# Attention and a mixture of experts on one core: the opening's order, and the gate weights' engine

## The chip, the cores and the metric

The kernel runs on one core of a Trainium2 chip. The core has TensorE (PE), VectorE (DVE), ScalarE (ACT), GpSimd (POOL) and SyncE (SP), which here only issues DMAs. Each engine works through its own instructions in the order in which the program lists them and waits at an instruction until the semaphores that it needs have come. The metric is the device time of one execution in microseconds, the median over runs.

## The reference

```python
# 2 batches x 8 heads, S = 1152, D = 64; q and k are 8 times a normal draw of 0.1
q_pool = q.reshape(B, H, S // 2, 2, D).mean(axis=3)          # 576 pooled queries
scores = np.matmul(q_pool, k.transpose(0, 1, 3, 2)) / np.sqrt(D)
attn = softmax(scores)                                         # with 1e-09 in the sum
x = np.matmul(attn, v)                                         # -> [1152 tokens, 512]
p = domain_probs / (domain_probs.sum(-1, keepdims=True) + 1e-09)
for e in range(4):                                             # all experts, dense
    out += p[:, e:e + 1] * (np.maximum(x @ w1[e], 0.0) @ w2[e])
```

## The kernel before

Two heads make a pair; there are eight pairs, and the pooled queries of a pair make nine **tiles** i = 0 to 8 of 128 rows, numbered through as g = 9n + i. The matmuls on q, k and the weights take fp32r operands, and to keep precision each operand is split into a high part `hi` (a rounded copy) and a low part `lo` (the value less `hi`). The split costs a copy and a subtraction for every operand, and which engine does them is one of the things that the change moves.

A tile goes through these steps, for which the text uses the letters:

- **S(g)**: six matmuls (nine for i = 8) in TensorE, three chunks of 384 keys into the one PSUM tile `spt` (L314). There is one `spt`, so S(g+1) can't begin before N(g) has read it.
- **N(g)**: VectorE negates and scales the scores into SBUF and takes the minimum (L317).
- **E(g)**: ScalarE's exponential with its sum (L323).
- **T(g)**: 18 half transposes of the exponentials in TensorE (L202, tile `pt`), two PSUM tiles from a pool of two; ScalarE copies the first out (L339), VectorE the second (L337).
- **PV**: TensorE's product with v (L352, tile `po`), spread over later tiles.

The main loop for tile g issues T(g), E(g+1), a part of PV, preparations, and then S(g+2) and N(g+2). The preparations for the next pair are `prep_q` (12 transposes, a copy by ScalarE, splits in POOL, four DMAs that stack `hi` and `lo`), and `prep_k` 1 and 2 (eight transposes each, a copy out of PSUM, a split in POOL, four DMAs). What `prep_k` transposes has first to be joined by POOL from the two heads' rows (`join_k`, L251, into `qsf` or `raw`). For the first pair the table `PREP0` puts them in tiles 2, 3 and 4, for later pairs `PREP` in tiles 0, 2 and 4. The PSUM pool of two (`ps_t`) that T uses is also that of these transposes.

Pair 0 has a way of its own. Its first four q blocks (the first **q chunk**) are added, transposed and split ahead of the k of the first head (`prep_q0(0)`, L222 and L223); the second chunk follows in tile 0 and the last block in tile 1, split by ScalarE and VectorE straight from PSUM. k is split in its row layout (`split_k0`, L228 and L229), transposed (L235) and copied out (L238). POOL adds the rest of q in one instruction (L177).

The gate weights p (`gate_weights`, L489 to L495, two pieces of 36 columns at the end) are computed once, after tile 13, by VectorE.

Order is written by hand: nothing moves instructions but the order of the code. DMAs go through SP's queue, also in that order. After the attention come the experts' matmuls (L135 and L669), in which TensorE is busy nearly all the time.

## Time and profile before

| what | us |
|---|---|
| median of 3 runs | 651.31 (650.85 to 651.96) |
| the profiled execution | 650.89 |
| its span in the trace | 649.1 |
| TensorE busy in the span | 628.1 |
| first 40 us: tiles 0 to 6 of pair 0 | see the rows below |

A row of the timeline gives the start and duration in us, the engine, the line of the program, the operation, what it writes and reads, and in brackets how long its engine stood idle before and what ended that. "DVE L317 [0.71 <-PE spt L314]" is then: VectorE idle for 0.71 us until TensorE's scores came. A row with x6 merges six instructions. A row of the windows gives for each engine the busy time in the stretch and the number of instructions, then the granted clock of TensorE as a share of 2.4 GHz.

### The profile page before, as it was taken

Reading aid. Unit: us, or ns where it says so; the run is one execution under the profiler, and the core shown is the slowest. Engines: PE = TensorE matmul, PEld = TensorE weight load, DVE = VectorE, ACT = ScalarE, POOL = GpSimd, SP = SyncE. Lnnn points to the kernel's source line nnn. Section 1 sums busy time; section 2 is a strip of 40 time slices with the busy share of each in tenths; the row PEclk is TensorE's granted clock in tenths of the full one; section 3 lists DMA queues with packets and bytes.
Section 4 is the critical chain, followed back from the end, with each engine's and each line's share of the span. In section 5 each row is a group of like instructions: output and inputs, shape, how many; then the busy total and the mean of one; then the engine's idle time right before and its main releaser. Section 6 shows DMA issues by size and latency. Waiting matters only on the chain.

```text
span 649.1 us, 12072 instructions
## 1 busy us (share of the span) xinstructions
PE 628.1 (97%) x4828; PEld 518.8 (80%) x4828; DVE 356.6 (55%) x544; ACT 306.9 (47%) x510; POOL 340.5 (52%) x398
## 2 busy tenths in 40 slices
PE   7599999999999999999999999999999999999997
PEld 6466667676776767798899899899899889989976
DVE  5466766566665666744544544544454454454454
ACT  4467677766666677461441351352243144135030
POOL 3335253436372478685844854774584484485140
PEclk8899999999999999999999999999999999999999
DMA  6744544636272621121211211212111121120105
GB/s 218 166 121 109 142 119 131 151 98 172 78 191 61 170 69 34 33 66 33 66 33 33 66 34 35 63 33 58 40 49 51 33 65 33 34 66 0 33 1 145
DMA packets 41782, 50.87 MB, mean 78 GB/s; under 512 B 3712, under 2 KB 27520, under 8 KB 41728
## 3 DMA queue, kind: packets, MB, share of 16 engines
q1 hardware_dynamic: 40928, 48.94, 28.1%
q10 hardware_dynamic: 800, 1.18, 0.5%
q8 instruction: 38, 0.62, 0.4%
q14 instruction: 16, 0.13, 0.1%
HBM read 30.97 MB, written 2.36 MB: 51 GB/s over the span
## 4 chain that ended last, share of the span: by engine, by line
PE 90%; DVE 4%; ACT 3%; issue 1%; POOL 1%; DVEq 0%; POOLq 0%; ACTq 0%
PE p L669 30%; PE spt L314 12%; PE po L352 12%; PE chy L135 11%; PE chx L135 8%; PE chz L135 8%; PE pt L202 7%; DVE sx L317 2%; ACT sx L323 2%; PE pr L370 1%; PE pk L202 1%; PE pq L202 1%; PE warm L445 1%; DVE acc L673 0%; ACT xr L598 0%
## 5 line engine op out<-in xcount | busy, mean ns | idle before, releaser
L669 PE MATMUL p<-w2s,hb 128*128 128x512 f32 (+1 forms) x870 | 199.2, 388 | 1.1 <-DVE acc L673 0.9
L669 PEld LDWEIGHTS p<-w2s,hb 128*128 128x128 f32 x870 | 161.8, 188 | 34.2 <-issue 1.3
L673 DVE SCALAR_TENSOR_TENSOR acc<-p,pw,acc 128x512 f32<-128x512 f32 (+1 forms) x136 | 101.5, 747 | 82.7 <-PE p L669 82.7
L317 DVE TENSOR_SCALAR_CACHE_REDUCE sx<-spt 128x1152 f32<-128x1152 f32 x72 | 97.7, 1357 | 78.5 <-PE spt L314 70.2
L116 POOL TENSOR_TENSOR kk<-kq,kk 128x512 fp32r<-128x512 f32 x64 | 72.5, 1161 | 117.9 <-ACT kk L108 117.9
L314 PE MATMUL spt<-kk,q2all 128*128 128x384 f32 x456 | 101.0, 358 | 3.7 <-DVE sx L317 3.2
L323 ACT ACTIVATE sx<-sx,mn 128x1152 f32<-128x1152 f32 x72 | 90.6, 1259 | 23.1 <-DVE sx L317 21.4
L314 PEld LDWEIGHTS spt<-kk,q2all 128*128 128x128 f32 x456 | 77.6, 192 | 20.1 <-DVE sx L317 16.3
L352 PE MATMUL po<-aT,vn 128*64 128x320 f32 (+1 forms) x576 | 86.2, 422 | 0.0
L600 POOL TENSOR_TENSOR hb<-xr,hb 128x576 fp32r<-128x576 f32 x48 | 68.6, 1432 | 21.9 <-ACT hb L599 21.9
L637 ACT ACTIVATE xr<-chx 128x576 f32<-128x576 f32 x15 | 9.8, 651 | 147.5 <-PE chx L135 147.5
L339 ACT ACTIVATE aT<-pt 128x640 f32<-128x640 f32 x72 | 50.7, 704 | 54.7 <-PE pt L202 54.7
L202 PEld LDWEIGHTS pt<-ident,sx 64*128 64x128 f32 x1296 | 46.7, 140 | 22.2 <-ACT sx L323 10.1
L202 PE MATMUL pt<-ident,sx 64*128 64x64 f32 x1296 | 57.1, 230 | 2.9 <-DVE aT L337 1.1
L135 PE MATMUL chx<-xa,kk 128*128 128x288 f32 x384 | 56.4, 296 | 1.3 <-ACT xr L514 0.5
L135 PEld LDWEIGHTS chx<-xa,kk 128*128 128x128 f32 x384 | 53.4, 189 | 3.3 <-ACT xr L514 1.0
L352 PEld LDWEIGHTS po<-aT,vn 128*64 128x64 f32 x576 | 35.4, 137 | 20.3 <-issue 0.7
L337 DVE COPY aT<-pt 128x512 f32<-128x512 f32 x72 | 49.2, 683 | 2.4 <-PE pt L202 2.3
L95 POOL TENSOR_TENSOR kq<-kq 128x256 f32<-128x256 f32 x64 | 45.8, 737 | 7.5 <-DMA kq<-in_moe_w_dram 6.3
L598 ACT ACTIVATE xr<-xr 128x576 f32<-128x576 f32 x48 | 32.9, 686 | 34.1 <-DVE xr L596 34.1
L135 PE MATMUL chy<-xb,kk 128*128 128x288 f32 x288 | 46.7, 298 | 0.1
L135 PE MATMUL chy<-q2all,kk 128*128 128x288 f32 x256 | 44.2, 295 | 0.0
(100 smaller groups left out, 671.7 us busy)
## 6 DMA issues: line engine op xcount, KB each, us to landing
kq<-in_moe_w_dram SPq DMA_DIRECT2D x64, 128.0 KB, 2.4
qsf<-in_moe_w_dram SPq DMA_DIRECT2D x16, 512.0 KB, 3.7
q2all<-q2all SPq DMA_DIRECT2D x28, 256.0 KB, 4.8
vn<-in_v_dram SPq DMA_DIRECT2D x8, 576.0 KB, 5.3
kk<-kk SPq DMA_DIRECT2D x28, 160.0 KB, 2.6
kq<-in_q_dram SPq DMA_DIRECT2D x7, 576.0 KB, 7.4
kq<-in_k_dram SPq DMA_DIRECT2D x7, 576.0 KB, 4.1
kk<-kk SPq DMA_DIRECT2D x28, 128.0 KB, 4.6
```

The costliest lines, as they stand in the source:

```text
L116: nc.gpsimd.tensor_tensor(flat(w1s[u % 2][:, 1, a:b]), flat(wf[:, a:b]), flat(w1s[u % 2][:, 0, a:b].bitcast(F32)), ALU.subtract)
L135: nc.tensor.matmul(chain[:, c, :CW], w1s[u % 2][:, a, WI[wo], kt, :], xop(xo, z, kt)[:, c * CW:(c + 1) * CW], start=(first and kt == 0 and ...
L202: nc.tensor.transpose(pt[:, a, j, :], src[r], ident[r, r])
L314: nc.tensor.matmul(spt[g][:, c, :NC], w, x, start=(j == 0), stop=(j == len(ops) - 1))
L317: nc.vector.tensor_scalar(sx[g % 3].rearrange("p (c x) -> p c x", c=3), spt.pop(g)[:, :, :NC], -INV, None, ALU.mult, ALU.min, accum_out=mn ...
L323: nc.scalar.activation(sx[g % 3], sx[g % 3], AF.Exp, bias=mn[g % 3], scale=-1.0, accum_out=sums[n % 2][:, i:i + 1])
L337: nc.vector.tensor_copy(dst, pt)
L339: nc.scalar.activation(dst, pt, AF.Copy)
L352: nc.tensor.matmul(po[h * HALF:(h + 1) * HALF, :w], vn[n % 2][:, h, kt, :], aT[grp][:, h, kt, :], start=(kt == 0), stop=(kt == KT - 1))
L600: nc.gpsimd.tensor_tensor(lo, c, hi.bitcast(F32), ALU.subtract)
L669: nc.tensor.matmul(pc, h[:, a, sl, ts_], w[:, b, sl, c0:c1], start=(m == 0), stop=(m == len(ops) - 1))
L673: nc.vector.scalar_tensor_tensor(ac, pc, pw[:, tt, e:e + 1], ac, ALU.mult, ALU.add)
```

## The change

Four things change, all in pair 0 but the last:

1. **Opening.** The split of k (first head) stands ahead of the split of q's first chunk in ScalarE and VectorE. The q transposes keep their place.
2. **Second q chunk and last block.** Blocks 4 to 8 are transposed together in tile 0 (ten transposes), copied to `raw` by VectorE in one piece, and split by POOL. Nothing of them is left in tile 1. The stacking DMAs, the sum of the next pair's q (`add_q`) and `join_k(0)` and `join_k(1)` follow S(2) in tile 0.
3. **Preparations for pair 1.** `PREP0` has tiles 3, 4 and 5 rather than 2, 3 and 4. `prep_q` no longer joins k rows for pair 1, and `prep_k` copies into a free part of `xr` rather than `raw`. The load of the k rows of pair 2 follows in tile 5.
4. **Gate weights.** The product and the two copies (L492, L495) run in POOL; the sum, the addition and the reciprocal stay in VectorE.

```diff
@@ -209,18 +209,26 @@
             nc.gpsimd.tensor_scalar(hi, src, 1.0, 1.0, ALU.mult, ALU.mult)
             nc.gpsimd.tensor_tensor(lo, src, hi.bitcast(F32), ALU.subtract)
 
-        def prep_q0(c):
-            ts_ = range(4 * c, min(4 * c + 4, 9))
-            pt = half_transposes("pq", [qs[:, t].rearrange("p z d -> p (z d)") for t in ts_], ps_s if c == 0 else None)
-            if c == 2:
-                for a, r in enumerate(ROWS):
-                    nc.scalar.activation(q2m[0][r, 0, r], pt[r, a, 0], AF.Copy)
-                for a, r in enumerate(ROWS):
-                    nc.vector.tensor_tensor(q2m[0][r, 1, r], pt[r, a, 0], q2m[0][r, 0, r].bitcast(F32), ALU.subtract)
-                return
-            hi, lo = [q2[0][:, z, :, 256 * c:256 * c + 256].rearrange("p s (t x) -> p s t x", x=HALF) for z in range(2)]
-            nc.scalar.activation(hi, pt, AF.Copy)
-            nc.vector.tensor_tensor(lo, pt, hi.bitcast(F32), ALU.subtract)
+        def transposes_q0(ts_, pool=None):
+            return half_transposes("pq", [qs[:, t].rearrange("p z d -> p (z d)") for t in ts_], pool)
+
+        def q_split(hi, lo, src):
+            nc.scalar.activation(hi, src, AF.Copy)
+            nc.vector.tensor_tensor(lo, src, hi.bitcast(F32), ALU.subtract)
+
+        def parts_q0(c):
+            return [q2[0][:, z, :, 256 * c:256 * c + 256].rearrange("p s (t x) -> p s t x", x=HALF) for z in range(2)]
+
+        def prep_q0():
+            pt = transposes_q0(range(4, 9))
+            src = raw[:, :10 * HALF].rearrange("p (a k x) -> p a k x", a=2, x=HALF)
+            nc.vector.tensor_copy(src, pt)
+            pool_split(*parts_q0(1), src[:, :, :4])
+            split_q2m(0, src)
+
+        def split_q2m(n, src):
+            for a, r in enumerate(ROWS):
+                pool_split(q2m[n % 2][r, 0, r], q2m[n % 2][r, 1, r], src[r, a, 4])
 
         def split_k0(h, c):
             t0, t1 = TCH[c]
@@ -275,16 +283,16 @@
                     dst = q2[n % 2].rearrange("p z s (y x) -> p (z s) y x", y=2)[r, :, y, :]
                     st = stq.rearrange("p z s j x -> p (z s) (j x)")[y * HALF:(y + 1) * HALF]
                     nc.sync.dma_start(dst.bitcast(F32), st.bitcast(F32))
-            for a, r in enumerate(ROWS):
-                pool_split(q2m[n % 2][r, 0, r], q2m[n % 2][r, 1, r], src[r, a, 4])
+            split_q2m(n, src)
             ab = kab[n % 2]
             pool_split(halves(ab[:, 0], 8, 9)[:, :, 0], halves(ab[:, 1], 8, 9)[:, :, 0], src[:, :, 5])
-            join_k(1)
+            if n > 1:
+                join_k(1)
 
         def prep_k(n, c):
             t0, t1 = KTS[c]
             pt = half_transposes("pk", [kc[c][:, (t - t0) * P:(t - t0 + 1) * P] for t in range(t0, t1)])
-            src = raw[:, :4 * P]
+            src = raw[:, :4 * P] if n > 1 else xr[:, 3, :4 * P]
             if c == 1:
                 join_k(2)
                 nc.vector.tensor_copy(halves(src, 0, 4), pt)
@@ -444,11 +452,12 @@
         for _ in range(NWARM):
             nc.tensor.transpose(warm[:, :P], ident, ident)
         add_q0(nc.vector, 0, 4)
-        prep_q0(0)
+        pq = transposes_q0(range(4), ps_s)
         split_k0(0, 0)
         ev = [prep_k0(0, 0)]
         split_k0(0, 1)
         ev.append(prep_k0(0, 1))
+        q_split(*parts_q0(0), pq)
         for fn in ev:
             fn()
         S_chunk(0, 0)
@@ -472,7 +481,7 @@
                  4: (0, 0, 0, 2), 5: (0, 0, 2, 4), 6: (0, 0, 4, 6), 7: (0, 0, 6, 8), 8: (0, 0, 8, 9)}
         SPREAD = {7: (0, 0), 1: (-1, 1)}
         PREP = {0: [(prep_q,)], 2: [(prep_k, 1)], 4: [(prep_k, 2)]}
-        PREP0 = {2: [(prep_q,)], 3: [(prep_k, 1)], 4: [(prep_k, 2)]}
+        PREP0 = {3: [(prep_q,)], 4: [(prep_k, 1)], 5: [(prep_k, 2)]}
 
         def pv_part(g):
             n, i = divmod(g, 9)
@@ -489,10 +498,10 @@
             nc.vector.tensor_reduce(prs, pr, AX.X, ALU.add)
             nc.vector.tensor_scalar_add(prs, prs, 1e-9)
             nc.vector.reciprocal(prs, prs)
-            nc.vector.tensor_tensor(pr, pr, prs.unsqueeze(2).to_broadcast([P, 18, E]), ALU.mult)
+            nc.gpsimd.tensor_tensor(pr, pr, prs.unsqueeze(2).to_broadcast([P, 18, E]), ALU.mult)
             for a in range(2):
                 sl = slice(a * HALF, (a + 1) * HALF)
-                nc.vector.tensor_copy(pw[sl], pr[sl, a:a + 17:2, :])
+                nc.gpsimd.tensor_copy(pw[sl], pr[sl, a:a + 17:2, :])
 
         for g in range(NTL):
             n, i = divmod(g, 9)
@@ -515,17 +524,12 @@
             pv_part(g)
             if i in SPREAD and n + SPREAD[i][0] >= 0:
                 spread_sums(n + SPREAD[i][0], SPREAD[i][1])
+            if g == 0:
+                prep_q0()
             if n + 1 < NP:
-                if g < 2:
-                    prep_q0(g + 1)
-                if g == 0:
-                    stack_k0()
-                if g == 1:
-                    add_q(nc.gpsimd)
-                    join_k(0)
                 for fn, *args in (PREP if n else PREP0).get(i, []):
                     fn(n + 1, *args)
-                if i == 4 and n + 2 < NP:
+                if i == (4 if n else 5) and n + 2 < NP:
                     load_kv(kn, k, n + 2)
             elif i == 7:
                 chx = ps_s.tile([P, 3, 512], F32, tag="s", name="chx")
@@ -535,6 +539,11 @@
                 for kt in range(2):
                     product(0, 2, kt, chx, False)
             scores(g + 2)
+            if g == 0:
+                stack_k0()
+                add_q(nc.gpsimd)
+                join_k(0)
+                join_k(1)
             if i == 3:
                 inv_sums(n, 0)
             if (n, i) == (1, 4):
```

ScalarE at the start of the program, first before and then changed (`kq` holds the rows of q and k, `kk` the split and transposed k, `q2all` the split q, `pq` and `pk` are PSUM tiles):

```order
L222 ACTIVATE q2all<-pq 128x2x256
L228 ACTIVATE kk_74<-kq 128x5x64
L228 ACTIVATE kk_74<-kq 128x4x64
L238 ACTIVATE kk_73<-pk 128x640
L228 ACTIVATE kk_74<-kq 128x5x64
```

```order
L236 ACTIVATE kk_74<-kq 128x5x64
L236 ACTIVATE kk_74<-kq 128x4x64
L216 ACTIVATE q2all<-pq 128x2x256
L246 ACTIVATE kk_73<-pk 128x640
L236 ACTIVATE kk_74<-kq 128x5x64
```

The high part of k now stands ahead of that of q; all else in the engine keeps its place.

TensorE in tiles 0 to 4 of pair 0, before and then changed (`pt<-ident,sx` is T, `spt` is S, `po` is PV, `pq` and `pk` are transposes of q and k):

```order
L202 MATMUL pt<-ident,sx_90 128x64 x18
L202 MATMUL pq<-ident,qsf 128x64 x8
L314 MATMUL spt<-kk_73,q2all 128x384 x6
L202 MATMUL pt<-ident,sx_91 128x64 x18
L202 MATMUL pq<-ident,qsf 128x64 x2
L314 MATMUL spt<-kk_73,q2all 128x384 x6
L202 MATMUL pt<-ident,sx_92 128x64 x18
L202 MATMUL pq<-ident,qsf 128x64 x10
L202 MATMUL pq<-ident,raw 128x64 x2
L314 MATMUL spt<-kk_73,q2all 128x384 x6
L202 MATMUL pt<-ident,sx_90 128x64 x18
L202 MATMUL pk<-ident,qsf 128x64 x8
```

```order
L202 MATMUL pq<-ident,qsf 128x64 x10
L322 MATMUL spt<-kk_73,q2all 128x384 x6
L202 MATMUL pt<-ident,sx_91 128x64 x18
L322 MATMUL spt<-kk_73,q2all 128x384 x6
L202 MATMUL pt<-ident,sx_92 128x64 x18
L322 MATMUL spt<-kk_73,q2all 128x384 x6
L202 MATMUL pt<-ident,sx_90 128x64 x18
L202 MATMUL pq<-ident,qsf 128x64 x10
L202 MATMUL pq<-ident,raw 128x64 x2
L322 MATMUL spt<-kk_73,q2all 128x384 x6
L202 MATMUL pt<-ident,sx_91 128x64 x18
L360 MATMUL po<-aT_93,vn_88 64x256 x4
```

Ten transposes of q stand in tile 0 (the second piece begins right behind T(0)), the preparation of pair 1's q is one tile later, and the first `pk`, which came after T(3), follows T(4) and its PV.

POOL after the sum of q's later blocks, before and then changed (64x64 are the two halves of the last q block, 128x128 into `kk` the ninth k block, `qsf<-kq 128x512` is `join_k`):

```order
L177 TENSOR_TENSOR qsf<-kq 128x640
L184 TENSOR_TENSOR qsf<-kq 128x2x4x64
L188 TENSOR_TENSOR qsf<-kq 128x128
L251 COPY raw<-kq 128x128
L209 TENSOR_SCALAR q2all<-raw 128x512
L210 TENSOR_TENSOR q2all<-raw,q2all 128x512
L209 TENSOR_SCALAR q2all<-raw 64x64
L210 TENSOR_TENSOR q2all<-raw,q2all 64x64
L209 TENSOR_SCALAR q2all<-raw 64x64
L210 TENSOR_TENSOR q2all<-raw,q2all 64x64
L209 TENSOR_SCALAR kk_74<-raw 128x128
L210 TENSOR_TENSOR kk_74<-raw,kk_74 128x128
```

```order
L177 TENSOR_TENSOR qsf<-kq 128x640
L209 TENSOR_SCALAR q2all<-raw 128x2x256
L210 TENSOR_TENSOR q2all<-raw,q2all 128x2x256
L209 TENSOR_SCALAR q2all<-raw 64x64
L210 TENSOR_TENSOR q2all<-raw,q2all 64x64
L209 TENSOR_SCALAR q2all<-raw 64x64
L210 TENSOR_TENSOR q2all<-raw,q2all 64x64
L184 TENSOR_TENSOR qsf<-kq 128x2x4x64
L188 TENSOR_TENSOR qsf<-kq 128x128
L259 COPY raw<-kq 128x128
L259 COPY qsf<-kq 128x512
L209 TENSOR_SCALAR q2all<-raw 128x512
```

Six instructions that split pair 0's own q are new at the front; `join_k(1)`, which stood behind the last row of the first list, now stands ahead of the splits of pair 1's q.

## Rows read from the trace of the kernel before

**Rows 1.** The page, part 1: busy us (share of the span) and instructions

```profile
PE 628.1 (97%) x4828; PEld 518.8 (80%) x4828; DVE 356.6 (55%) x544; ACT 306.9 (47%) x510; POOL 340.5 (52%) x398
```

**Rows 2.** Windows: each engine's busy us and instructions, PEclk granted, DMA share, GB/s

```profile
8.00:8.50 0.50, 0.15 (x1) 0.15 (x1) 0.50 (x1) 0.50 (x2) 0.50 (x1) 0.80 0.07 28
...
20.00:25.00 5.00, 4.00 (x56) 2.86 (x55) 3.43 (x6) 3.71 (x9) 0.21 (x1) 1.00 0.85 189
...
30.00:35.00 5.00, 5.00 (x38) 3.69 (x34) 2.98 (x6) 1.70 (x2) 2.90 (x4) 0.50 0.82 193
...
35.50:36.00 0.50, 0.50 (x11) 0.43 (x9) 0.00 (x0) 0.00 (x0) 0.00 (x0) 0.89 0.87 205
```

**Rows 3.** Timeline of the opening: start us, us, engine, line, tile, idle before

```profile
1.19 0.89 SPq L173 DMA_DIRECT2D kq<-in_k_dram  x2
...
5.17 0.60 ACT L222 ACTIVATE q2all<-pq 128x512 fp32r<-128x512 f32 x1 [3.16 <-PE pq L202]
...
5.66 0.77 ACT L228 ACTIVATE kk<-kq 128x320 fp32r<-128x320 f32 x2
...
6.40 0.82 DVE L229 TENSOR_TENSOR kk<-kq,kk 128x320 fp32r<-128x320 f32 x2
...
7.60 0.70 ACT L238 ACTIVATE kk<-pk 128x640 fp32r<-128x640 f32 x1 [1.17 <-PE pk L235]
...
7.94 0.69 DVE L238 CAST kk<-pk 128x512 fp32r<-128x512 f32 x1 [0.72 <-PE pk L235]
...
8.35 2.29 PE L314 MATMUL spt<-kk,q2all 128*128 128x384 f32 x6 [0.46 <-ACT kk L238]
...
10.68 1.36 DVE L317 TENSOR_SCALAR_CACHE_REDUCE sx<-spt 128x1152 f32<-128x1152 f32 x1 [0.71 <-PE spt L314]
```

**Rows 4.** DMA issues, window 1.15 to 1.3 us: KB, us to landing

```profile
kq<-in_k_dram SPq DMA_DIRECT2D x1, 288.0 KB, 3.1
```

**Rows 5.** Timeline, POOL in the opening

```profile
7.74 1.55 POOL L177 TENSOR_TENSOR qsf<-kq 128x640 f32<-128x640 f32 x1 [5.57 <-DMA kq<-in_q_dram]
```

**Rows 6.** Source view of L229: duration ns min/median/max

```profile
L229 DVE TENSOR_TENSOR kk<-kq,kk x4: 410/450/946, 6.4 to 9.6; 128x320 fp32r<-128x320 f32 x2, 128x256 fp32r<-128x256 f32 x2
```

**Rows 7.** Timeline of tiles 1 to 4, VectorE

```profile
13.72 1.36 DVE L317 TENSOR_SCALAR_CACHE_REDUCE sx<-spt 128x1152 f32<-128x1152 f32 x1 [1.07 <-PE spt L314]
...
16.99 0.69 DVE L223 TENSOR_TENSOR q2all<-pq,q2all 128x512 fp32r<-128x512 f32 x1 [1.30 <-ACT q2all L222]
...
21.19 1.36 DVE L317 TENSOR_SCALAR_CACHE_REDUCE sx<-spt 128x1152 f32<-128x1152 f32 x1
...
23.98 1.36 DVE L317 TENSOR_SCALAR_CACHE_REDUCE sx<-spt 128x1152 f32<-128x1152 f32 x1 [0.82 <-PE spt L314]
```

**Rows 8.** Timeline of tile 3, POOL and who waits

```profile
24.79 0.62 POOL L209 TENSOR_SCALAR q2all<-raw 128x512 fp32r<-128x512 f32 x1 [8.65 <-ACT raw L270]
...
25.49 1.27 POOL L210 TENSOR_TENSOR q2all<-raw,q2all 128x512 fp32r<-128x512 f32 x1
...
28.94 0.61 POOL L251 COPY qsf<-kq 128x512 f32<-128x512 f32 x1
...
29.60 0.69 PE L202 MATMUL pk<-ident,qsf 64*128 64x64 f32 x8 [4.38 <-POOL qsf L251]
```

**Rows 9.** Timeline, TensorE in tiles 5 and 7

```profile
37.17 0.78 PE L202 MATMUL pt<-ident,sx 64*128 64x64 f32 x18
...
45.53 1.29 PE L314 MATMUL spt<-kk,q2all 128*128 128x384 f32 x6
```

**Rows 10.** Timeline, gate weights

```profile
70.08 0.97 DVE L492 TENSOR_TENSOR pr<-pr,prs 128x72 f32<-128x72 f32 x1
...
72.24 0.47 PE L202 MATMUL pt<-ident,sx 64*128 64x64 f32 x8 [1.14 <-DVE aT L337]
```

**Rows 11.** DMA issues L263, windows 40.5 to 41 and 61.4 to 61.6 us

```profile
kk<-kk SPq DMA_DIRECT2D x1, 160.0 KB, 2.7
...
kk<-kk SPq DMA_DIRECT2D x1, 128.0 KB, 5.7
```

## The prediction

> **What bounds the kernel now.** The page first: TensorE is busy for 628.1 of 649.1 us [rows 1], so this change can only save idle time of TensorE and time at its lower clock. Both lie in the first pair. The windows of the granted clock come second: 1.00 (2.4 GHz) nearly everywhere, but falling to 0.50 (1.2 GHz) after 8.0, and 0.50 from 30 to 35 us, back at 35.5 to 36 [rows 2]. Third, the timeline of the opening, read for what each wait ends on. S(0) begins at 8.35, released by ScalarE's copy of the transposed k, and its six matmuls take 2.29 us at the low clock [rows 3] where S(9) takes 1.29 [rows 9]. In tiles 1 and 2 VectorE waits 1.30 us for ScalarE's half of the q split, and N(2) stands behind that [rows 7]. In tile 3 TensorE waits 4.38 us for `join_k(1)`, which POOL reaches only after all splits of pair 1's q [rows 8]; the low clock follows. From tile 5 on TensorE has hardly a gap, so a start that is earlier there is kept to the end. The one later gap that the change touches is 1.14 us behind the gate weights [rows 10].
>
> **Opening: k ahead of q.** The k rows of the first head land at 1.19 + 3.1 = 4.3 [rows 3, 4], but ScalarE takes them at 5.66, behind q's high part, which itself waits until 5.17 for TensorE [rows 3]. Changed, k's high part can run from 4.3 to 5.1 and its low part on VectorE (two times about 0.4) until 5.7; q's parts keep 5.17 and 5.8 to 6.5, as their wait is on TensorE. So the nine k transposes end at about 6.35 and no longer after 7.6. ScalarE's copy (0.70) follows q's high part, 6.0 to 6.7, and S(0) begins at 6.75: 1.6 us earlier. If the landing slips to 5.0, k's high part pushes q's back and 1.0 us is left; more than 1.6 isn't to be had, since q's high part waits for TensorE.
>
> TensorE was idle from 5.1, when ScalarE took over from it, to 6.9, when the first low part of k was done [rows 3], and then the clock fell. Now it is idle for some 0.3 us there and again 0.4 before S(0), so I take S(0) at full clock: another 1.0 us (2.29 against 1.29). N(0) then begins at 10.68 - 2.5 = 8.2. The bounds for the clock are 0 and 1.0; I take 1.0, as tiles 1 to 3 kept the full clock with TensorE busy for 4.00 of 5 us [rows 2], and the new opening is about as busy.
>
> **Second q chunk through POOL.** From N(0) to N(1) nothing changes (10.68 to 13.72, 3.05): N(1) at 11.25. N(1) to N(2) took 3.9 and N(2) to N(3) 3.6 us, each with a piece of q between; N(3) to N(4), with none, 2.79 [rows 3, 7]. That is the chain S, N, S through the one `spt`. Changed, tile 0 has ten transposes (0.4) ahead of S(2): N(2) at 14.4, N(3) 17.2, N(4) 20.0. VectorE's copy of 640 columns is new; nothing shows it, but ScalarE takes 0.70 for 640 and VectorE 0.69 for 512 [rows 3], so it lies between 0.7 and 0.9. It runs beside S(2) and costs nothing; if S(2) didn't cover it, 0.2. POOL's split (0.62 and 1.27 as in [rows 8]) ends at about 16.2 and is needed by S(4) at 18.6. Behind it POOL has some 4 us of work (q's last block, `add_q`, the two joins) until 20.2; the transposes of `prep_q` come at 21.4. Both are covered by more than a microsecond.
>
> **Joined k rows and the later preparations.** `pk` 1 finds its rows ready, so the 4.38 us wait goes, and with it the idle time ahead of the second low-clock stretch. `prep_q`'s 12 transposes stand ahead of S(5): N(5) at 23.4. Then TensorE is the bound: T(4) 0.78, PV about 1.0, `pk` 0.4, S(6) 1.3, and T(5) begins at 26.75, where it began at 37.17 [rows 9].
>
> What is late next is POOL. ScalarE's copy for `prep_q` ends at 23.7 (N(4), E(4) and 0.8). From the start of the splits to the join it took 4.15 us (24.79 to 28.94); one copy of 0.4 for the sums now stands ahead of `join_k(2)`, which ends at 23.75 + 4.15 + 0.4 + 0.6 = 28.9. TensorE wants `pk` 2 at 28.45, after T(5) and PV: a stall of 0.5. POOL's split of `pk` 1 (2.0 with its gaps) ends at 31.0; only then can ScalarE copy `pk` 2 into the same part of `xr` (0.6), and the second half of T(6), which needs the PSUM tile that this copy empties, waits until 31.7 where TensorE would be there at 31.1: 0.6. Queued behind that copy on ScalarE stands E(7), needed only 3 us later. Bounds of both stalls: 0 and, if POOL runs 10% slower over these 7 us, 1.9; I take 1.2 (rounded up).
>
> From T(5) to S(9) it took 8.36 us [rows 9]. Now `pk` 2 (0.4) and the stalls come to it: S(9) at 26.75 + 8.36 + 0.4 + 1.2 = 36.7 and not 45.53, **8.8 us earlier**. The stacking DMAs of `pk` 2, also a tile later, must not end after that: the second of them is issued at 33.8 and lands 2.7 later [rows 11], at 36.5, and S(9) reads what it brings in its second chunk, at 37.1. The load of pair 2's k rows, also queued a tile later on SP, keeps over 2 us ahead of its join.
>
> **Gate weights.** VectorE drops L492 (0.97) and two copies (0.4). The copy behind them moves from 71.5 to 70.1, and T(15)'s second half no longer waits 1.14 us for it: **1.25** with the hand-over. POOL takes three small instructions, at a time when what follows is not wanted for over 5 us.
>
> One row speaks against a part of the change, in the opening again. One of the four L229 took 946 ns, where the median is 450; the last of them starts at 9.6, so the long one lies beside POOL's L177, 7.74 to 9.29 [rows 5, 6]. Changed, L229 of the second head runs at 7.1 to 7.9, and its second piece begins at about 7.5, 0.25 us ahead of L177. If POOL comes first, that piece waits until 9.29 and N(0) with it: 1.55 us.
> The Trainium skill says as much (SBUF — State Buffer, "Who interferes with whom"): a VectorE instruction with two SBUF inputs and a GpSimd one that reads SBUF need the same port, and the one that begins first keeps it to its end. By that rule the trace's 946 ns is a blocked instruction, and the order of the two starts decides between the sum above and the second case below.
>
> **Sum.** 8.8 + 1.25 = 10.05. The profiled execution took 650.89 (its span of 649.1 and 1.8 around it, which stay), so 640.85; the median of the runs shown is 0.42 above it, which makes **641.3**.
>
> **The rivals.**
> - POOL's L177 comes before VectorE's second piece: 1.55 lost, 642.8. For it, the margin of 0.25 between two estimates; against it, that L177 waits for a DMA, which the change doesn't move.
> - The clock falls all the same. In the opening it gives back 1.0 (642.3). Or POOL's stalls in tiles 5 and 6 bring it down as the long wait did: that stretch ran to 35.5 from 29.6, about 3 us lost, 644.3. Against it: those stalls are 1.2 us and not 4.4.
> - The stacking DMAs land late. 5.7 us have been seen [rows 11] where other loads run; then S(9) waits some 2.4 us: 643.7. For it, a margin of 0.6; against it, that nothing else is queued then.
> - POOL is not the pacer of tiles 5 and 6, the stalls vanish: 640.1.
> - The change doesn't do what it says at the gate weights: TensorE finds another wait there, and the 1.25 is gone: 642.5.
> - Slower than before: the denser opening works at half clock throughout, since no stretch in it is free of waits. From 8.2 to S(9) TensorE has about 24 us of work at full rate (eight T at 0.78, eight S at 1.3 to 1.8, four PV at 1.0 and some 2 of q and k transposes), so 24 lost, 14 in all: 665. It decides from 10 us of such work on. Against it, the full clock in tiles 1 to 3 with as many gaps, and that the clock came back in under 7 us even after the long wait.
>
> **How the numbers follow.** The forecast, 641.3 (640.6 to 642.0 with the small bounds), has 0.42; L177 first 0.2; the clock 0.15, two thirds of it in the opening; late DMAs 0.08; no POOL stalls 0.07; the gate weights 0.05; slower 0.03. The range from 639.8 to 644.4 leaves out the slower case, a part of the clock's, and combinations of two losses, together under 0.2. A measurement of this kernel can tell about 0.2% (1.3 us) from no change. All cases but the last are faster by 6 us or more; some misreading of the path may cost the whole gain. Faster 0.95, the same 0.02, slower 0.03.
>
> **What would show it.** S(0) at 6.7 to 6.9 with six matmuls in 1.3 to 1.5 us and the clock at 1.00 to 35 us; N starts 2.8 to 3.2 apart from N(1) to N(4); no wait of `pk` 1 on POOL; short waits (0.3 to 0.8) of `pk` 2 on `join_k(2)` and of T(6) on ScalarE's copy; S(9) at 36 to 38; no gap behind the gate weights. Wrong would be an L229 of over 0.9 us, a clock of 0.50 anywhere, or S(9) waiting for a DMA.

## The result and the profile after

The changed kernel takes **641.65 us** (640.62 to 641.79, four runs) where the kernel before takes 651.63 beside it (650.85 to 652.32): the ratio is 0.9844, interval 0.9827 to 0.9861. That is faster by about 10 us, and 0.35 above the forecast of 641.3. The profiled execution took 641.72 with a span of 639.9.

The page's first line of the changed kernel, to stand beside [rows 1]:

```profile
PE 625.5 (98%) x4828; PEld 517.1 (81%) x4828; DVE 356.0 (56%) x539; ACT 306.2 (48%) x507; POOL 344.3 (54%) x407
```

Span less busy time of TensorE was 21.0 us and is 14.4: 6.6 us of idle time are gone, and 2.6 of busy time, about what the low-clock stretch of [rows 2], 30 to 35 us, can have cost. Where this happened is seen best on the starts of N(g) in VectorE, read from the timelines of the two profiled executions (us):

| | N(0) | N(1) | N(2) | N(3) | N(4) | N(5) | N(9) | N(15) | N(16) | N(71) | span |
|---|---|---|---|---|---|---|---|---|---|---|---|
| before | 10.68 | 13.72 | 17.60 | 21.19 | 23.98 | 32.55 | 46.96 | 67.72 | 72.11 | 256.92 | 649.1 |
| changed | 9.59 | 12.61 | 15.73 | 18.60 | 21.53 | 24.79 | 39.32 | 60.19 | 63.24 | 247.94 | 639.9 |
| earlier by | 1.09 | 1.11 | 1.87 | 2.59 | 2.45 | 7.76 | 7.64 | 7.53 | 8.87 | 8.98 | 9.2 |

The opening gives 1.1 (forecast 2.5), the tiles up to N(4) 1.4 (forecast 1.5), the joined rows with the clock and what POOL takes back 5.2 (forecast 4.8, as S(9) was to be 8.8 earlier), the gate weights 1.34 (forecast 1.25). From tile 16 on the two traces run alike but for 0.3 us.

The timeline of the changed opening answers [rows 3, 5] (columns as there; L236, L246, L322, L237 and L325 are the old L228, L238, L314, L229 and L317):

```profile
4.42 0.78 ACT L236 ACTIVATE kk<-kq 128x320 fp32r<-128x320 f32 x2 [2.41 <-DMA kq<-in_k_dram]
4.53 0.69 PE L202 MATMUL pq<-ident,qsf 64*128 64x64 f32 x8
...
4.92 0.83 DVE L237 TENSOR_TENSOR kk<-kq,kk 128x320 fp32r<-128x320 f32 x2 [0.64 <-ACT kk L236]
...
5.47 1.38 PE L243 MATMUL pk<-identr,kk 128*128 128x128 f32 x9 [0.25 <-DVE kk L237]
...
6.38 0.70 ACT L246 ACTIVATE kk<-pk 128x640 fp32r<-128x640 f32 x1 [0.52 <-PE pk L243]
...
7.14 2.29 PE L322 MATMUL spt<-kk,q2all 128*128 128x384 f32 x6 [0.29 <-ACT kk L246]
...
7.50 2.17 DVE L237 TENSOR_TENSOR kk<-kq,kk 128x320 fp32r<-128x320 f32 x2
...
7.70 1.69 POOL L177 TENSOR_TENSOR qsf<-kq 128x640 f32<-128x640 f32 x1 [5.52 <-DMA kq<-in_q_dram]
...
9.59 1.34 DVE L325 TENSOR_SCALAR_CACHE_REDUCE sx<-spt 128x1152 f32<-128x1152 f32 x1
```

k's high part does begin at 4.42, when it lands. But S(0) takes 2.29 us, as it did before, and VectorE's two subtractions of the second head take 2.17 us where two took 0.83 in the first. By the rows S(0) ends at 9.43 and the subtractions at 9.67, and N(0) begins at 9.59 (the rows of neighbours on an engine overlap by up to a tenth).

The windows of the same stretch (columns as in [rows 2]) must be read with care:

```profile
5.00:10.00 5.00, 4.46 (x28) 3.99 (x24) 4.55 (x7) 2.16 (x5) 1.69 (x1) 1.00 0.49 153
10.00:15.00 5.00, 3.80 (x43) 2.97 (x42) 3.94 (x7) 3.75 (x5) 0.00 (x0) 1.00 0.92 303
```

They give a granted clock of 1.00, but S(0)'s six matmuls take 2.29 us, the same as in [rows 3] at a granted 0.50, and the second head's k transposes at 9.23 are as slow as those at 5.47, 0.15 us each. At the full rate, [rows 9] has 1.29 for an S. The view says 1.00 in every 10 us of this trace up to 630 us, so it doesn't show the difference; the durations say that TensorE worked at the lower of its two levels, 1.2 GHz, to about 10 us. In the kernel before, the same q transposes and the first k transposes took 0.59 and 0.96 us, where the changed kernel has 0.69 and 1.38:

```profile
4.53 0.59 PE L202 MATMUL pq<-ident,qsf 64*128 64x64 f32 x8
...
6.94 0.96 PE L235 MATMUL pk<-identr,kk 128*128 128x128 f32 x9 [1.82 <-DVE kk L229]
```

The tiles, against [rows 7 to 9] (`pk` is line 202 still):

```profile
14.49 0.81 DVE L225 COPY raw<-pq 128x640 f32<-128x640 f32 x1
...
15.73 1.36 DVE L325 TENSOR_SCALAR_CACHE_REDUCE sx<-spt 128x1152 f32<-128x1152 f32 x1 [0.43 <-PE spt L322]
...
26.44 0.46 PE L202 MATMUL pk<-ident,qsf 64*128 64x64 f32 x8
...
30.23 0.46 PE L202 MATMUL pk<-ident,qsf 64*128 64x64 f32 x8 [0.24 <-POOL qsf L259]
...
32.16 0.60 ACT L300 ACTIVATE xr<-pk 128x512 f32<-128x512 f32 x1 [0.99 <-POOL kk L210]
...
32.81 0.46 PE L202 MATMUL pt<-ident,sx 64*128 64x64 f32 x8 [0.42 <-ACT xr L300]
...
37.90 1.29 PE L322 MATMUL spt<-kk,q2all 128*128 128x384 f32 x6
```

No VectorE wait for ScalarE's q is left, the first `pk` (26.44) waits for nothing, the second (30.23) 0.24 us for `join_k(2)`, ScalarE's copy of it 0.99 for POOL's split, and T(6)'s second half 0.42 for that copy. S(9) begins at 37.90 and not at 45.53.

The gate weights, against [rows 10]:

```profile
62.31 0.63 DVE L345 COPY aT<-pt 128x512 f32<-128x512 f32 x1
...
62.47 0.32 POOL L501 TENSOR_TENSOR pr<-pr,prs 128x72 f32<-128x72 f32 x1 [0.41 <-DVE prs L500]
...
63.05 0.77 PE L202 MATMUL pt<-ident,sx 64*128 64x64 f32 x18
```

VectorE's copy follows the reciprocal directly, and T(15) runs in one piece without a wait.

### The profile page after: what moved, and what is told of

Read it like the earlier page. It is cut to its first block, busy times and chain, and to the rows that moved or that the text cites. A ratio compares the mean times of both kernels' runs of the same rounds, so it can differ in the third digit from the quotient of the medians.

```text
span 639.9 us, 12066 instructions
## 1 busy us (share of the span) xinstructions
PE 625.5 (98%) x4828; PEld 517.1 (81%) x4828; DVE 356.0 (56%) x539; ACT 306.2 (48%) x507; POOL 344.3 (54%) x407
## 4 chain that ended last, share of the span: by engine, by line
PE 89%; DVE 3%; ACT 2%; DMA 2%; POOL 1%; issue 1%; SPq 1%; DVEq 0%; ACTq 0%; POOLq 0%
PE p L678 31%; PE spt L322 12%; PE chy L135 12%; PE po L360 11%; PE chx L135 8%; PE chz L135 8%; PE pt L202 6%; DVE sx L325 2%; ACT sx L331 1%; DMA kk<-kk 1%; PE pr L378 1%; DMA kq<-in_q_dram 1%; PE pk L202 1%; PE pq L202 0%; DVE acc L682 0%
## 5 line engine op out<-in xcount | busy, mean ns | idle before, releaser
L325 DVE TENSOR_SCALAR_CACHE_REDUCE sx<-spt 128x1152 f32<-128x1152 f32 x72 | 97.7, 1357 | 78.8 <-PE spt L322 67.7
L322 PE MATMUL spt<-kk,q2all 128*128 128x384 f32 x456 | 100.0, 355 | 4.2 <-DVE sx L325 3.1
L322 PEld LDWEIGHTS spt<-kk,q2all 128*128 128x128 f32 x456 | 76.8, 190 | 20.3 <-DVE sx L325 15.2
```

Of the source, the lines that this page charges most:

```text
L322: nc.tensor.matmul(spt[g][:, c, :NC], w, x, start=(j == 0), stop=(j == len(ops) - 1))
L325: nc.vector.tensor_scalar(sx[g % 3].rearrange("p (c x) -> p c x", c=3), spt.pop(g)[:, :, :NC], -INV, None, ALU.mult, ALU.min, accum_out=mn ...
```

## The experiments

Each was run beside the kernel before; its ratio to that is given with the 95% interval. The starts of N come from its one profiled execution.

| run | edit, on the changed kernel but for the third | us, median (range) | ratio to before | N(0) | N(9) | N(16) |
|---|---|---|---|---|---|---|
| e1_gate_dve | gate weights on VectorE | 645.47 (643.24 to 646.52) | 0.9902 (0.9878 to 0.9926) | 9.21 | 41.02 | 66.18 |
| e2_q_first | q split ahead of k | 644.30 (642.90 to 645.99) | 0.9881 (0.9855 to 0.9907) | 11.20 | 43.32 | 67.24 |
| e3_before_join | kernel before, rows joined early | 646.33 (645.28 to 646.91) | 0.9918 (0.9899 to 0.9936) | 10.74 | 41.78 | 66.94 |
| e4_no_lock | POOL's addition held back | 640.87 (640.69 to 641.89) | 0.9839 (0.9823 to 0.9855) | 8.16 | 37.96 | 61.88 |
| f1_after | none | 641.94 (641.89 to 643.61) | 0.9860 (0.9834 to 0.9885) | 9.44 | 39.22 | 63.14 |
| f2_no_lock_two_buf | held back, second part of `xr` | 641.24 (640.72 to 642.00) | 0.9842 (0.9821 to 0.9862) | 9.56 | 39.10 | 63.04 |
| f3_q_from_psum | q's second chunk not through POOL | 644.68 (644.18 to 645.65) | 0.9895 (0.9875 to 0.9916) | 9.02 | 41.28 | 65.09 |
| f4_prep_early | preparations in tiles 2, 3, 4 | 641.50 (640.46 to 643.21) | 0.9847 (0.9823 to 0.9872) | 8.27 | 37.74 | 61.68 |
| g1_all_three | held back, second part, early tiles | 639.94 (639.72 to 640.89) | 0.9832 (0.9818 to 0.9847) | 8.51 | 37.34 | 61.23 |
| g2_all_three_fill | the same and two idle transposes | 639.65 (639.60 to 639.96) | 0.9823 (0.9810 to 0.9837) | 8.32 | 37.15 | 61.06 |
| h1_fill | two idle transposes | 641.25 (640.44 to 645.20) | 0.9853 (0.9828 to 0.9877) | 9.43 | 39.21 | 63.11 |
| h2_fill_no_lock | two idle transposes, held back | 640.81 (640.50 to 641.06) | 0.9837 (0.9823 to 0.9852) | 8.49 | 38.31 | 62.25 |

### The gate weights on VectorE again

```diff
-            nc.gpsimd.tensor_tensor(pr, pr, prs.unsqueeze(2).to_broadcast([P, 18, E]), ALU.mult)
+            nc.vector.tensor_tensor(pr, pr, prs.unsqueeze(2).to_broadcast([P, 18, E]), ALU.mult)
...
-                nc.gpsimd.tensor_copy(pw[sl], pr[sl, a:a + 17:2, :])
+                nc.vector.tensor_copy(pw[sl], pr[sl, a:a + 17:2, :])
```

> The changed kernel with the gate weights' product and copies back on VectorE. Theory (the gate weights are worth what TensorE waited there, 1.25 us): TensorE waits 1.0 to 1.2 us for VectorE's copy in tile 15, and the time is 642.9, 1.25 above the changed kernel's 641.65. Rival (that wait was hidden by another one behind it): the time stays within 0.3 of 641.65.

From N(15) to N(16) it took 4.27 us and in the changed kernel 3.05: 1.22 for the gate weights, and the table of waits from 55 to 75 us (engine, line, what it waited for; us in total, times, longest) has the wait back:

```profile
PE pt L202 <- DVE aT L345: 1.0, 1, 1.0
```

The time was 645.47, 2.6 more than the 642.9 expected. In the profile the rest comes from the opening, and shows what can happen there in the changed kernel too, since nothing was altered in it. The one of the four executions whose mean granted clock was 1.000 took 643.24; the others (0.989 to 0.994) took 645.28 to 646.52.

```profile
6.72 1.32 PE L322 MATMUL spt<-kk,q2all 128*128 128x384 f32 x6 [0.46 <-ACT kk L246]
...
7.04 1.56 POOL L177 TENSOR_TENSOR qsf<-kq 128x640 f32<-128x640 f32 x1 [4.87 <-DMA kq<-in_q_dram]
...
7.06 2.23 DVE L237 TENSOR_TENSOR kk<-kq,kk 128x320 fp32r<-128x320 f32 x2
...
9.09 0.93 PE L243 MATMUL pk<-identr,kk 128*128 128x128 f32 x9 [1.06 <-DVE kk L237]
```

The windows behind it (columns as in [rows 2]):

```profile
10.00:15.00 5.00, 3.85 (x35) 3.01 (x34) 3.13 (x6) 3.25 (x5) 0.00 (x0) 0.64 0.95 316
15.00:20.00 5.00, 4.60 (x34) 3.77 (x30) 2.79 (x4) 2.38 (x5) 3.48 (x7) 0.68 1.03 224
```

Here S(0) runs at full clock, 1.32 us. But POOL's addition and VectorE's subtractions meet, TensorE waits 1.06 us for the second piece, and from 11.4 to 18.2 us the clock is recorded at half: N(2) comes at 17.43 and not at 15.73.

### q ahead of k again

```diff
+        q_split(*parts_q0(0), pq)
         split_k0(0, 0)
         ev = [prep_k0(0, 0)]
         split_k0(0, 1)
         ev.append(prep_k0(0, 1))
-        q_split(*parts_q0(0), pq)
```

> The changed kernel with the split of the first q chunk ahead of the split of k again, as before. Theory (the order is worth the 1.1 us by which N(0) came earlier): N(0) at 10.7 and 642.7. Rival (what holds N(0) is the low clock of S(0) and VectorE's blocked subtraction, not the order): N(0) within 0.3 of the 9.59 of the changed kernel, 641.7.

N(0) came at 11.20, 1.6 later than in the changed kernel, and the time was 644.30, some 2.5 us more than its two measurements. S(0) itself begins 1.73 later (8.87 and 7.14), of which 0.17 is a later start of the q transposes (4.70 and 4.53): so the order alone is worth close to the 1.6 us of the prediction. In time the theory has the sign; its size, 1.0 us, is that of two of the four executions (642.90 and 643.11). The other two took 645.49 and 645.99, and the profile is of the last of these. In it TensorE stayed at the low level for longer. S(1) shows it, 2.26 us for six matmuls, where the changed kernel needs 1.48, a wait included:

```profile
8.87 2.29 PE L322 MATMUL spt<-kk,q2all 128*128 128x384 f32 x6 [0.29 <-ACT kk L246]
...
12.71 2.26 PE L322 MATMUL spt<-kk,q2all 128*128 128x384 f32 x6 [0.45 <-DVE sx L325]
```

Its S(2) at 17.32 took 2.29 us as well. Whether the sparser opening or only this execution kept the clock low isn't shown.

### Only the joined rows, on the kernel before

At the end of `prep_q`, in `prep_k`, and in tile 1:

```diff
-            join_k(1)
+            if n > 1:
+                join_k(1)
...
-            src = raw[:, :4 * P]
+            src = raw[:, :4 * P] if n > 1 else xr[:, 3, :4 * P]
...
                     join_k(0)
+                    join_k(1)
```

> The kernel before with one thing added: the next pair's k rows are joined early (in tile 1) and their PSUM copies go to the free part of xr; the order of the opening, the q pieces and the tiles of the preparations stay. Theory (the wait of 4.4 us and the low clock behind it go, and POOL's splits then hold the second k piece and T(5) for about 1 us each): TensorE no longer waits for the first join, the clock stays at 1.00 at 30 to 35 us, N(5) comes 5 to 6 us earlier than before, and the time is 646.3. Rival (the preparations have to move a tile as well, since POOL's queue turns the wait into another of nearly the same length): 649.5 or more.

646.33 against 646.3 expected. N(5) came 5.26 earlier than before and N(9) 5.18, with an opening that took as long as before (N(0) at 10.74). The first `pk` waits 0.26, the second 0.73 for the join, T(5) 0.43 for ScalarE's copy; at 30 to 35 us the clock is at 1.00, where [rows 2] has 0.50. The timeline of TensorE and the window:

```profile
25.53 0.46 PE L202 MATMUL pk<-ident,qsf 64*128 64x64 f32 x8 [0.26 <-POOL q2all L209]
...
29.71 0.46 PE L202 MATMUL pk<-ident,qsf 64*128 64x64 f32 x8 [0.73 <-POOL qsf L251]
...
32.30 0.46 PE L202 MATMUL pt<-ident,sx 64*128 64x64 f32 x8 [0.43 <-ACT xr L293]
```

```profile
30.00:35.00 5.00, 4.57 (x46) 3.28 (x42) 2.04 (x3) 2.64 (x6) 4.45 (x6) 1.00 0.84 196
```

So this edit alone carries 5.2 of the 9.2 us. The rival, that the tiles of the preparations must move as well, falls.

### The two caps on N(0)

```diff
+        nc.gpsimd.tensor_copy(spread[:, :1], khl[:, 1, 8, 1, :1].bitcast(F32))
         add_q0(nc.gpsimd, 4, 9)
```

> The changed kernel, with POOL's addition of the later q blocks held back until VectorE has done its last subtraction for the second head's k (a one-column copy ahead of it reads that result), so that the two no longer meet. Theory A (VectorE's blocked subtraction holds N(0)): no subtraction of over 0.6 us, N(0) at 8.2 to 8.6, 640.4. Theory B (S(0) at half clock ends at 9.43 and holds N(0) all by itself): no subtraction of over 0.6 us either, but N(0) at 9.5, 641.6.

Without the meeting the two subtractions took 0.83, and N(0) came at 8.16, as the prediction had it:

```profile
6.79 1.33 PE L322 MATMUL spt<-kk,q2all 128*128 128x384 f32 x6 [0.46 <-ACT kk L246]
...
7.13 0.83 DVE L237 TENSOR_TENSOR kk<-kq,kk 128x320 fp32r<-128x320 f32 x2
...
8.16 1.36 DVE L325 TENSOR_SCALAR_CACHE_REDUCE sx<-spt 128x1152 f32<-128x1152 f32 x1 [0.20 <-PE spt L322]
...
8.26 1.55 POOL L177 TENSOR_TENSOR qsf<-kq 128x640 f32<-128x640 f32 x1
```

That looked like theory A, but S(0) also took 1.33 us here: the clock was up. Two causes changed at once, the time (640.87) is within a microsecond of the changed kernel's, and the next runs had to part them.

> The changed kernel once more, unaltered, beside the runs that follow. If the level of the clock in the opening differs from execution to execution, its times spread over 640.3 to 643.5 us and the profile shows S(0) in either 1.3 us (full clock) or 2.3 (half); if it is a property of the kernel, S(0) takes 2.3 us again and the times stay within 640.6 to 641.8.

The unaltered kernel again: 641.89 to 643.61, so the spread is nearer to the first expectation and S(0), 2.29 us again, to the second. There is a meeting once more, in which each waits for the other in turn (POOL's addition 1.87 us rather than 1.55, VectorE's pair 2.18):

```profile
6.98 2.29 PE L322 MATMUL spt<-kk,q2all 128*128 128x384 f32 x6 [0.29 <-ACT kk L246]
...
7.33 2.18 DVE L237 TENSOR_TENSOR kk<-kq,kk 128x320 fp32r<-128x320 f32 x2
...
7.36 1.87 POOL L177 TENSOR_TENSOR qsf<-kq 128x640 f32<-128x640 f32 x1 [5.19 <-DMA kq<-in_q_dram]
```

The clock's rise differs between executions with the same opening: up to S(0) the code of e1 is that of this kernel, and there the k transposes took 0.96 us and not 1.38. It isn't a matter of the chip either: f1 and f2, at the low level, and f3 and f4, where the clock came up, ran on the same one.

```diff
-            src = raw[:, :4 * P] if n > 1 else xr[:, 3, :4 * P]
+            src = raw[:, :4 * P] if n > 1 else xr[:, 3, (c - 1) * 4 * P:c * 4 * P]
```

The addition held back as in e4, and a second part of `xr` for `pk` 2:

> The changed kernel with POOL's addition held back as in the run without the meeting, and with a second part of xr for pair 1's second k piece, so that ScalarE's copy need not wait until POOL has split the first. Theory (POOL paces tiles 5 and 6 through that one buffer): TensorE's wait of 0.42 for ScalarE in tile 6 goes, S(9) comes 0.4 to 0.5 earlier than without the second part, and the time is 640.4. Rival (the split itself is late, so the wait moves on to the stacking DMAs ahead of S(9)): no wait in tile 6, but one of 0.3 to 0.5 at S(9), and 640.9 as without it.

For the opening this run is the missing corner: no meeting, but the low clock. N(0) stands at 9.56, as with the meeting (S(0) began 0.1 to 0.26 later here, as k landed later; from its start it is 2.32 us to N(0), and 2.45 with the meeting):

```profile
7.24 2.29 PE L322 MATMUL spt<-kk,q2all 128*128 128x384 f32 x6 [0.29 <-ACT kk L246]
...
7.59 0.82 DVE L237 TENSOR_TENSOR kk<-kq,kk 128x320 fp32r<-128x320 f32 x2
...
9.56 1.36 DVE L325 TENSOR_SCALAR_CACHE_REDUCE sx<-spt 128x1152 f32<-128x1152 f32 x1 [1.15 <-PE spt L322]
```

The two idle transposes were tried to bring the clock up in every execution, first in a run with other edits (below), and then by themselves. `fill(1)` is one transpose of the identity into `warm`, behind the q transposes and behind the first k transposes:

```diff
+        def fill(m):
+            for _ in range(m):
+                nc.tensor.transpose(warm[:, :P], ident, ident)
...
         pq = transposes_q0(range(4), ps_s)
+        fill(1)
         split_k0(0, 0)
         ev = [prep_k0(0, 0)]
         split_k0(0, 1)
         ev.append(prep_k0(0, 1))
+        fill(1)
```

> The changed kernel with the two idle transposes in the opening alone; POOL's addition may meet VectorE's subtractions. Theory (the low clock and the meeting each hold N(0), so taking one away leaves the other): S(0) in 1.3 us, but a subtraction of over 0.6 us beside POOL's addition and N(0) at 9.0 to 9.4, and 641.3. Rival (the clock is all of it): N(0) at 8.2 to 8.6, and 640.4.

> The changed kernel with the two idle transposes and with POOL's addition held back. Both theories: S(0) in 1.3 us, no subtraction of over 0.6 us, N(0) at 8.2 to 8.5. By the theory this is 0.8 to 1.0 below the run with the transposes alone, 640.4; by the rival it equals it.

With the transposes and the meeting S(0) takes 1.32 us, TensorE then waits 0.96 for the blocked subtraction, and N(0) is at 9.43; with the meeting taken away as well (second list), N(0) is at 8.49:

```profile
6.98 1.32 PE L322 MATMUL spt<-kk,q2all 128*128 128x384 f32 x6 [0.33 <-ACT kk L246]
...
7.32 2.18 DVE L237 TENSOR_TENSOR kk<-kq,kk 128x320 fp32r<-128x320 f32 x2
...
7.57 1.66 POOL L177 TENSOR_TENSOR qsf<-kq 128x640 f32<-128x640 f32 x1 [5.40 <-DMA kq<-in_q_dram]
...
9.65 0.50 PE L243 MATMUL pk<-identr,kk 128*128 128x128 f32 x4 [0.96 <-DVE kk L237]
```

```profile
7.14 1.32 PE L322 MATMUL spt<-kk,q2all 128*128 128x384 f32 x6 [0.32 <-ACT kk L246]
...
7.64 0.83 DVE L237 TENSOR_TENSOR kk<-kq,kk 128x320 fp32r<-128x320 f32 x2 [0.22 <-ACT kk L236]
```

| N(0) at, and in brackets from the start of S(0) | addition meets the subtractions | it does not |
|---|---|---|
| S(0) at half clock (2.29 us) | 9.59 (2.45), 9.44 (2.46) (changed kernel, twice) | 9.56 (2.32) (f2) |
| S(0) at full clock (1.31 to 1.42 us) | 9.21 (2.49) (e1), 9.43 (2.45) (h1), 9.02 (2.25) (f3) | 8.16 (1.37) (e4), 8.27 (1.40) (f4), 8.49 (1.35) (h2), 8.51 (1.36) and 8.32 (1.35) (g1, g2) |

The bracketed numbers leave out that S(0) itself begins at 6.72 to 7.24, as k lands earlier or later and the k transposes are faster or slower. Each cause alone holds N(0) 2.25 to 2.49 us behind the start of S(0), and both together 2.45; only with both gone is it 1.35 to 1.40. (In f4 the addition does begin while the second piece runs, and doesn't stretch it.) The theory that h1 was to test holds in the traces: 1.10 between h1 and h2 from the start of S(0) to N(0), 0.94 at N(0) itself, 0.90 at N(9). In the times the difference is 0.44 (641.25 and 640.81), with intervals that overlap, and the profiles can't say in how many of the other executions the two met.

The clock of every execution adds something that N(0) doesn't show. In the five kernels with the addition held back (e4, f2, g1, g2, h2) none of 21 executions has a mean granted clock below 0.998. Where the addition may meet the subtractions and nothing else slows tile 0 (the changed kernel twice, e1, f4, h1), six of 22 have 0.989 to 0.994, and they are the slowest of their runs (643.21 to 646.52). Only one of the six has a profile, e1's, in which the clock falls after the wait of 1.06 us; h1's profile has a wait of 0.96 and no fall. That the meeting brings the clock down in the other five is argued from these counts, not shown.

### Tiles 0 to 6

With the second part of `xr` (f2, its edit and expectation above) the wait of T(6) for ScalarE is gone, and S(9) waits 0.17 for a stacking DMA in its place:

```profile
38.01 0.96 PE L322 MATMUL spt<-kk,q2all 128*128 128x384 f32 x4 [0.17 <-DMA kk<-kk]
```

From N(0) to N(9) it gains 6.74 on the kernel before, against 6.48 without the second part (e4): 0.26, between theory and rival. The time, 641.24, settles nothing at this size.

```diff
-            nc.vector.tensor_copy(src, pt)
-            pool_split(*parts_q0(1), src[:, :, :4])
-            split_q2m(0, src)
+            q_split(*parts_q0(1), pt[:, :, :4])
+            for a, r in enumerate(ROWS):
+                q_split(q2m[0][r, 0, r], q2m[0][r, 1, r], pt[r, a, 4])
```

> The changed kernel, with q's second chunk and last block split by ScalarE and VectorE straight from PSUM, all in tile 0, so that POOL has none of it. Theory (ScalarE's part stands behind E(1), and VectorE's behind that holds N(2)): N(1) to N(2) takes 4.5 to 5.2 us rather than 3.1, and the time is 643.2 to 643.7, 1.5 to 2.0 above the changed kernel. Rival (the copy of 640 columns that POOL's way needs costs VectorE as much): N(1) to N(2) within 0.4 of 3.1, 641.7.

N(1) to N(2) took 5.00 us (3.12 in the changed kernel), since VectorE waits again for ScalarE's part behind E(1); 644.68, one us above the theory. TensorE waited 1.57 us, and the clock, 0.87 at 15 to 20 us and 0.79 at 20 to 25, was at half between tiles 2 and 3, which accounts for a part of the time:

```profile
15.30 0.69 DVE L217 TENSOR_TENSOR q2all<-pq,q2all 128x512 fp32r<-128x512 f32 x1 [1.30 <-ACT q2all L216]
...
17.15 0.46 PE L202 MATMUL pt<-ident,sx 64*128 64x64 f32 x8 [1.57 <-DVE q2all L217]
```

```diff
-        PREP0 = {3: [(prep_q,)], 4: [(prep_k, 1)], 5: [(prep_k, 2)]}
+        PREP0 = {2: [(prep_q,)], 3: [(prep_k, 1)], 4: [(prep_k, 2)]}
...
-                if i == (4 if n else 5) and n + 2 < NP:
+                if i == 4 and n + 2 < NP:
```

> The changed kernel with pair 1's preparations in tiles 2, 3 and 4 as before. Theory (POOL, which now splits pair 0's q first, reaches the sum and the join at 20.0 to 20.7, and T(2) ends at 19.2): TensorE waits about 1.4 us for the transposes of pair 1's q in tile 2, and the later steps get that back only in part, so the time is 642.2 to 643. Rival (it is POOL's chain that sets T(5) to S(9), and it starts a tile earlier): 640.5 to 641.2, faster than with the later tiles.

TensorE does wait in tile 2 for POOL's sum, 0.76 us, but it gets that back: from N(0) to N(9) 6.81 gained, against 6.46 to 6.55 with the later tiles. The rival is nearer, by 0.3 us in the trace; the times (641.50 and 641.94) don't part them.

```profile
18.77 0.69 PE L202 MATMUL pq<-ident,qsf 64*128 64x64 f32 x10 [0.76 <-POOL qsf L184]
```

### All together

> The changed kernel with POOL's addition held back, the second part of xr, and pair 1's preparations in tiles 2, 3 and 4. Theory (what each of them gave in its own trace adds up: 0.3 for the earlier tiles, 0.3 for the second part, up to 1.0 for the missing meeting, the last only in executions whose S(0) runs at full clock): from N(0) to N(9) the gain on the kernel before is 6.9 to 7.1 us, and the time is 640.6. Rival (they relieve the same wait of POOL's chain, so they do not add): 6.8 or less from N(0) to N(9), and 641.2 or more.

> The same three edits, with one idle transpose of the identity in TensorE behind the q transposes and one behind the first k transposes of the opening. They write a PSUM tile that nothing reads. Theory (the clock comes up early when TensorE has no gaps in the opening): S(0) at full clock, 1.3 us, N(0) at 8.2 to 8.7, and 640.0. Rival (when the clock comes up differs from execution to execution, whatever fills the gaps): S(0) in 1.3 or in 2.3 us, and a time within 0.5 of the same kernel without them.

639.94, and 639.65 with the idle transposes. From N(0) to N(9) the gain on the kernel before is 7.45, more than either expectation: with the second part of `xr` and the earlier tiles neither T(5) nor S(9) waits. g2's four runs lie within 0.36 us (S(0) in 1.31 us in its profile), and its time is below every run of the changed kernel (640.62 to 643.61). That its narrow range comes from the clock isn't shown, since only one execution has a profile. Nor do the idle transposes win over their rival: g1 without them had S(0) in 1.32 us too, and the two times differ by 0.29, with intervals that overlap.

## Why the prediction was right, and where it was not

- **k ahead of q.** S(0) was to begin at 6.75. With the clock up it begins at 6.72 and 6.79 (e1, e4), so the step is right, and e2 puts 1.6 us on the order by itself; in the changed kernel's own profile the nine k transposes take 1.38 us, where e4 has 0.96, and it begins at 7.14.
- **"I take S(0) at full clock: another 1.0 us."** This is the step that failed. It was read from the fall before S(0) in the kernel before, as if a denser opening could only keep a clock that was up. In the changed kernel it had not come up yet. The q transposes ahead, which the change doesn't touch, took 0.69 us there, 0.59 in the kernel before and 0.46 in e1. The first k transposes, 0.96 us in the kernel before, took 1.38 in the changed kernel (twice), f2 and e2, and S(0) ran at the low level as well (2.29 us); with the same code up to there they took 0.96 and S(0) 1.32 in e1 and e4. The forecast gave the clock's loss here a chance of 0.10, as a thing that the code decides; it varies from one execution to the next, and S(0) was low in three of the eight profiles of this opening without idle transposes.
- **The rival of the meeting came true and cost next to nothing here.** POOL's L177 came between the two pieces, as described, and VectorE's second piece waited for its end; it took 1.77 us, where an L229 of over 0.9 was named as a sign of being wrong. The margin of 0.25 was smaller than the spread of L177's own start, 6.86 to 7.79 us over the profiles in which it isn't held back. Its price of 1.55 was too high (1.1 from the start of S(0) to N(0) in e1 against e4 and in h1 against h2), and in an execution at low clock it is 0.1, as S(0) itself ends hardly sooner than the subtractions (f2 against the changed kernel). The two losses were taken as ones that add; they lie side by side. The rule that was weighed there (the Trainium skill, SBUF — State Buffer, "Who interferes with whom": the first to start keeps the port to its end) fits the traces: with POOL held back the pair took 0.82 or 0.83 rather than 1.99 to 2.23 us, and where VectorE's pair came just ahead (f4, with POOL starting 0.6 after it) it wasn't stretched.
- **Second q chunk through POOL.** N(1) to N(2) 3.12 (forecast 3.15), VectorE's copy 0.81 (0.7 to 0.9). f3 puts 1.9 us on it. N(3) to N(4) took 2.93 and not 2.79. TensorE stood idle for 0.80 us ahead of S(4), a wait that the profile lets POOL's addition (L184) end; what the 0.14 come from stays open.
- **Joined rows and POOL as the next pacer.** Right in mechanism and nearly in size: the stalls were 0.24 and 0.42, where 0.5 and 0.6 were taken, and T(5) to S(9) took 9.82 us, forecast 9.96. e3 shows the term by itself.
- **The tile later for the preparations.** The prediction left it uncosted, as something that the rest needs. It isn't needed: f4 does without, and is 0.3 us better between N(0) and N(9).
- **Gate weights.** 1.22 (e1) and 1.34, forecast 1.25.
- **The sum.** 10.05 forecast; 9.17 between the two profiled executions, 9.98 between the medians. The first lacks 1.4 us of the opening and 0.1 of the tiles up to N(4); 0.65 came back behind N(4). The forecast then added 0.42, by which the median of the kernel before stood above its profiled execution; the changed kernel's median stands 0.07 below its own. These 0.49 hide more than half of the 0.88 that was missing, so the closeness of 641.65 to 641.3 is in part luck.

## What to carry to other kernels

Where one engine does a queue of preparations, put first what the busiest engine will ask for first: moving one copy of 0.6 us ahead of 4 us of splits, with a buffer of its own for what follows, was worth about half of this change (e3). When two delays end at about the same point, taking one away shows nothing, so vary them together and apart before either is called harmless. Where one engine's instruction stretches another's (0.83 to 2.2 us here) and the order of their starts is a matter of tenths of a microsecond, hold one back by a dependency.

## What was not expected of the hardware

- The granted clock of the first microseconds can't be read from the windows: they show 1.00 in the changed kernel, while S(0) takes 2.29 us and not 1.32. At which of its levels TensorE works there differs between executions with the same code up to there, and with it the end of S(0) by a microsecond. Two idle transposes in the gaps went with a full clock at S(0) in all three profiles that had them (g2, h1, h2), but five of eight without them had it as well (e1, e4, f3, f4, g1).
- VectorE's product of 72 columns took 0.97 us in the kernel before [rows 10]. It ended 0.09 after POOL's addition beside it (first list below), and in e1 it took 0.97 and ended 0.09 after that addition again; POOL's own product takes 0.32. So most of the 0.97 was likely a wait, a reason for moving it that the prediction didn't name. Likewise a VectorE instruction on four columns (L369; its median is 0.16) took 0.99 us beside POOL's split in tile 4 of the changed kernel (second list), where TensorE didn't wait for it:

```profile
69.67 1.29 POOL L184 TENSOR_TENSOR qsf<-kq 128x512 f32<-128x512 f32 x1
```

```profile
25.77 1.28 POOL L210 TENSOR_TENSOR q2all<-raw,q2all 128x512 fp32r<-128x512 f32 x1
...
26.07 0.99 DVE L369 TENSOR_SCALAR rs<-sums 128x4 f32<-128x4 f32 x1
```
